# Sliding-window attention and channel mix on one core: another order of the three compute engines' lists

## The chip, the cores and the metric

The kernel runs on one core of one Trainium2 chip. The core has a matrix engine (PE), a vector engine (DVE), a scalar engine (ACT), a general engine (POOL) and a sync engine (SP). Each takes its own list of instructions in order and waits at the head of it. Here POOL and SP mostly issue DMA transfers. The metric is the time of one execution on the device in microseconds (us).

## What is computed

Attention over 8 batches, 8 heads, 576 positions and 64 values per head, with a linear bias by distance and a window of 128 positions; its output, with the heads side by side, goes through a channel mix with a hidden width of 1024.

```python
scores = scale * np.matmul(q, k.transpose(0, 1, 3, 2))
rel = pos[:, None] - pos[None, :]
bias = slopes[:, None, None] * (-np.abs(rel).astype(np.float32))[None, :, :]
mask = (rel >= 0) & (rel < window)
scores = np.where(mask, scores + bias[None], -1000000000.0)
attn = np.exp(scores - np.max(scores, axis=-1, keepdims=True))
attn = attn / (np.sum(attn, axis=-1, keepdims=True) + 1e-09)
x = np.matmul(attn, v)                    # then (B, S, H * D)
x_prev = np.concatenate([np.zeros((B, 1, D)), x[:, :-1, :]], axis=1)
xk = mu_k * x + (1.0 - mu_k) * x_prev
xr = mu_r * x + (1.0 - mu_r) * x_prev
k = np.maximum(xk @ w_k, 0.0)
v = k * k @ w_v
return 1.0 / (1.0 + np.exp(-(xr @ w_r))) * v
```

The multiplications take bf16 and sum in f32.

## The kernel before

**Attention.** A batch is worked in head pairs, numbered 0 to 3 in the text (g in the code). For each pair q and k are transposed, on PE (L398, out of qx or cb, with the identity ident or its f32 form id) or by DMA (L554, qx out of cb), and where PE does it a copy (L715) on ACT or DVE brings the result from PSUM to a buffer qk. PE computes scores for two heads (L742). In batch 0 the bias is added on PE by multiplying dist, the table of distances, with sid, a scaled identity per head (L748; DVE makes the eight sids at L687); from batch 1 on DVE multiplies with a mask instead (L779; the mask is made by ACT at L1198). ACT takes the exponential (L766, into at). PE multiplies with v and a column of ones (L395, vs or tv with at: the "attend"), and DVE divides (L813, L819, into xu). That result is transposed, on PE with a copy (L398, L715 into xt) or by DMA on SP (L928, xt out of xu), and DVE forms the shifted mixes (L906 into dl, L913 into xk and xr). Batch 0 is worked in two halves, so that PE has its first work early: four pairs of 768-wide exponentials for the first half, then the second half, whose scores have a 768-wide and a 512-wide part.

**Channel mix.** Two batches are 1152 rows, and they are worked in chunks of 512, 384 and 256 columns, the first of all in two chunks of 256. For each of eight groups of the hidden width PE multiplies xk with wk_sb (L395), ACT takes the relu (L1022, into rl), and DVE, or ACT in the early chunks, squares it (L996 and L994, into kk). For each 128 rows PE multiplies xr with wr_sb, ACT takes a tanh (L1040, into rs), PE multiplies kk with wv_sb, and DVE joins both (L1054, into one of five buffers ot), from where SP sends 256 KB out (L1079).

**Loads.** POOL issues nearly all loads in one fixed list: v, q, k, then wk_sb in two halves, further batches, wr_sb and wv_sb in two halves (L560). Only the first q and k of pairs 0 and 1 come through SP and ACT (L569, into qx), and DVE casts them (L715 CAST qx).

**PSUM.** There are eight banks, in four pairs (duo0 to duo3). One of them first holds the output of 82 small multiplications of a cleared buffer (L395, duo out of warm), which have no use but to keep PE at work; they are steps in PE's list like the others.

**What sets the order.** The program describes every piece of work as a step with its engine or engines, the steps it depends on, the buffers it takes and those it gives back. Each step for PE, ACT or DVE gets the next number when it is added, and a table ORDER holds for each of these engines the numbers in the order in which they are to run. Where a step may run on ACT or on DVE (many copies L715, the early squares), the list in which its number stands decides.

```python
        self.places = {n: (e, i) for e, ns in ORDER.items() for i, n in enumerate(ns)}
```

A run through all steps then takes for such an engine only the step that is next in its list (`n.place == turn[e]`) and gives it free buffers. POOL and SP take, of the steps that are ready in that run, the first by a written priority, so their lists follow from the others. The program is emitted in that order, and the chip's engines wait for each other by semaphores.

Of the kernel before, what the change touches and what calls it, by code (L numbers as in the profile page):

```python
# [20 lines left out]

ORDER = {
    "PE": [int(x) for x in """
# [17 lines left out]
""".split()],  # L41
    "ACT": [int(x) for x in """
# [11 lines left out]
""".split()],  # L54
    "DVE": [int(x) for x in """
# [16 lines left out]
""".split()],  # L72
}

# [1249 lines left out]
```

## Time and profile before

| What | Value |
|---|---|
| runs | median 227.4 us of 3 (226.96 to 227.56) |
| the profiled execution | 226.97 us |
| its span | 225.1 us; 1.87 us lie around it |
| busy | PE 217.7, DVE 186.8, ACT 153.0, POOL 91.9 us |
| last work of PE | ends 3.3 us ahead of the span's end |
| granted clock of PE | full in all 40 slices |

The span is the time that the trace covers. A row of a timeline gives the start in us from the span's start, how long the group took from first start to last end, engine, line, operation, what it writes and reads, the shape and the count; at its end, in brackets, how long the engine stood idle before and for what. Neighbouring groups of PE overlap in the rows, since its multiplications are pipelined: a start that follows soon after the last start is no loss.

### The profile page before, as it was taken

How to read it: one execution, taken by the hardware profiler on the slowest of the kernel's cores; microseconds unless marked ns; L12 is line 12 of the kernel's file. 1: busy time of each engine (PE TensorE's matmuls, PEld its weight loads, DVE VectorE, ACT ScalarE, POOL GpSimd, SP SyncE). 2: the span in 40 equal slices, each digit the busy share in tenths (PEclk: the TensorE clock that was granted, in tenths of full speed). 3: DMA queues.
4: the chain of work that ended last, by engine and by line, in shares of the span. 5: the costliest groups of instructions: out<-in, count | busy, mean ns of one | idle time of the engine just before them, and what ended most of it. 6: DMA issues, size and time to landing. Idle time of an engine off the chain costs nothing.

```text
span 225.1 us, 6344 instructions
## 1 busy us (share of the span) xinstructions
PE 217.7 (97%) x2525; PEld 131.5 (58%) x2555; DVE 186.8 (83%) x422; ACT 153.0 (68%) x276; POOL 91.9 (41%) x118
## 2 busy tenths in 40 slices
PE   8999999999999999999999999999999999999994
PEld 8666756756765555555665565446664655456542
DVE  5779898899768998999789996599969989957433
ACT  2488999898999886980899665843469654135801
POOL 8865726589980983374428663400000000000000
PEclk9999999999999999999999999999999999999999
DMA  7999999999999999999999999999952121243015
GB/s 169 177 186 200 195 197 175 227 146 178 185 154 148 161 149 156 150 182 133 207 207 142 152 181 155 148 180 191 206 167 76 51 57 30 79 155 126 3 41 192
DMA packets 132093, 33.85 MB, mean 150 GB/s; under 512 B 119256, under 2 KB 127712, under 8 KB 132064
## 3 DMA queue, kind: packets, MB, share of 16 engines
q0 software_dynamic: 95728, 16.26, 96.5%
q1 hardware_dynamic: 34592, 16.59, 36.6%
q10 hardware_dynamic: 1744, 0.59, 1.1%
q8 instruction: 20, 0.33, 0.6%
q14 instruction: 9, 0.07, 0.1%
HBM read 33.56 MB, written 9.44 MB: 191 GB/s over the span
## 4 chain that ended last, share of the span: by engine, by line
PE 91%; ACT 4%; DVE 2%; issue 1%; DVEq 0%
PE duo L395 77%; PE duo L742 7%; PE duo L398 4%; PE duo L748 2%; ACT at L766 1%; ACT xt L715 1%; ACT rl L1022 1%; ACT qk L715 1%; DVE ot L1054 1%; DVE qk L715 1%; ACT kk L994 0%; DVE at L779 0%; ACT rs L1040 0%; DVE tv L499 0%; DVE tt L715 0%
## 5 line engine op out<-in xcount | busy, mean ns | idle before, releaser
L1022 ACT ACTIVATE rl<-duo 128x256 bf16<-128x256 f32 (+2 forms) x104 | 47.3, 485 | 34.8 <-PE duo L395 25.1
L395 PE MATMUL duo<-xk,wk_sb 128*128 128x256 bf16 (+2 forms) x410 | 70.2, 312 | 0.3
L766 ACT ACTIVATE at<-duo 128x1024 bf16<-128x1024 f32 (+2 forms) x68 | 63.8, 987 | 8.9 <-PE duo L742 8.5
L395 PE MATMUL duo<-wv_sb,kk 128*128 128x512 bf16 (+2 forms) x281 | 66.1, 373 | 1.1 <-issue 0.5
L395 PEld LDWEIGHTS <-wk_sb 128*128 128x128 bf16 x416 | 38.9, 98 | 22.9 <-issue 0.8
L395 PEld LDWEIGHTS <-kk 128*128 128x128 bf16 x296 | 27.1, 98 | 29.8 <-issue 1.3
L779 DVE TENSOR_TENSOR at<-at,mask 128x1024 bf16<-128x1024 bf16 x56 | 37.2, 680 | 5.8 <-ACT at L766 5.7
L519 POOL DMA_DIRECT2D vs<-in_v_dram x32 | 28.4, 901 | 22.7 <-PE duo L395 16.8
L996 DVE TENSOR_TENSOR kk<-rl 128x256 bf16<-128x256 bf16 (+2 forms) x95 | 29.9, 336 | 8.4 <-ACT rl L1022 8.3
L395 PE MATMUL duo<-wr_sb,xr 128*128 128x512 bf16 x135 | 35.5, 379 | 0.5
L1040 ACT ACTIVATE rs<-duo 128x512 bf16<-128x512 f32 x36 | 21.6, 612 | 19.8 <-PE duo L395 17.1
L1054 DVE SCALAR_TENSOR_TENSOR ot<-rs,duo 128x512 f32<-128x512 bf16 (+2 forms) x37 | 24.3, 665 | 9.1 <-PE duo L395 8.9
L819 DVE TENSOR_TENSOR xu<-duo,rc 128x640 bf16<-128x640 f32 (+2 forms) x36 | 26.2, 738 | 0.4
L913 DVE SCALAR_TENSOR_TENSOR xk<-dl,mu_sb,xt 128x576 bf16<-128x576 bf16 (+1 forms) x32 | 24.6, 779 | 0.2
L913 DVE SCALAR_TENSOR_TENSOR xr<-dl,mu_sb,xt 128x576 bf16<-128x576 bf16 (+1 forms) x32 | 24.6, 778 | 0.0
L395 PEld LDWEIGHTS <-at 128*128 128x128 bf16 x576 | 21.5, 97 | 4.8 <-issue 0.3
L395 PE MATMUL duo<-vs,at 128*128 128x65 bf16 x512 | 21.7, 193 | 0.0
L395 PEld LDWEIGHTS <-xr 128*128 128x128 bf16 x144 | 13.3, 98 | 12.9 <-issue 0.4
L550 POOL DMA_DIRECT2D cb<-in_k_dram x20 | 17.8, 926 | 7.3 <-DMA vs<-in_v_dram 7.2
L550 POOL DMA_DIRECT2D cb<-in_q_dram x20 | 17.7, 931 | 5.6 <-DMA vs<-in_v_dram 2.5
L715 ACT COPY qk<-duo 128x512 bf16<-128x512 bf16 (+1 forms) x25 | 14.5, 593 | 0.4 <-PE duo L398 0.4
L906 DVE TENSOR_TENSOR dl<-xt 128x576 bf16<-128x576 bf16 (+1 forms) x32 | 13.4, 438 | 1.1 <-ACT xt L715 0.6
(73 smaller groups left out, 189.4 us busy)
## 6 DMA issues: line engine op xcount, KB each, us to landing
out_dram<-ot SPq DMA_DIRECT2D x34, 256.0 KB, 4.7
vs<-in_v_dram POOLq DMA_DIRECT2D x32, 128.0 KB, 8.5
cb<-in_q_dram POOLq DMA_DIRECT2D x20, 128.0 KB, 9.8
cb<-in_k_dram POOLq DMA_DIRECT2D x20, 128.0 KB, 11.2
wk_sb<-in_moe_w_k_dram POOLq DMA_DIRECT2D x2, 512.0 KB, 8.7
cb<-in_q_dram POOLq DMA_DIRECT2D x4, 256.0 KB, 9.7
cb<-in_k_dram POOLq DMA_DIRECT2D x4, 256.0 KB, 9.7
wv_sb<-in_moe_w_v_dram POOLq DMA_DIRECT2D x2, 512.0 KB, 12.2
```

What stands on the lines that cost most here:

```text
L395: return use(h, nc.tensor.matmul(*a, **k))
L519: return dma(POOL, 256, issue_t(1024), lambda e: nc.gpsimd.dma_start(out=vs_buf[h.idx][:, j, :, 0:D], in_=v[b, :, 128 * j:128 * j + 128].r ...
L550: return [dma(POOL, 256, issue_t(1024), lambda e, r=r: nc.gpsimd.dma_start(out=cb_buf[h.idx][:, i, r], in_=src[:, :, r]), [g], kind="q") f ...
L715: return (nc.scalar.copy if e == ACT else nc.vector.tensor_copy)(out=out, in_=in_)
L766: lambda e, ah=ah, w=w, hp=hp: nc.scalar.activation(out=ah(), in_=two(hp)[:, :, 0:w], func=AF.Exp, scale=float(scale)), (), [hp])
L779: nc.vector.tensor_tensor(out=a, in0=a, in1=m, op=ALU.mult)
L819: use(hp, nc.vector.tensor_tensor(out=out_, in0=a5()[:, :, :, 0:D], in1=rc[:, :, 0:nt, None].to_broadcast([128, 2, nt, D]), op=ALU.mult), hx)
L913: lambda e: nc.vector.scalar_tensor_tensor(out=buf[hk.idx][:, g, e0 + c0:e0 + c1], in0=dls(), scalar=mu[:, g:g + 1], in1=xc(1), op0=ALU.mu ...
L996: nc.vector.tensor_tensor(out=out, in0=in_, in1=in_, op=ALU.mult)
L1022: a = op(ACT, act_t(n), [s], pr, lambda e, hp=hp, hr=hr: use(hp, nc.scalar.activation(out=rl_buf[hr.idx][:, 0:n], in_=one(hp)[:, 0:n], fun ...
L1040: lambda e, hp=hp, hs=hs: use(hp, nc.scalar.activation(out=rs_buf[hs.idx], in_=one(hp), func=AF.Tanh, scale=0.5), hs), [hs], [hp])
L1054: use(hv, nc.vector.scalar_tensor_tensor(out=ot_buf[ho.idx][:, a:b], in0=rs_buf[hs.idx][:, a:b], scalar=1.0, in1=one(hv)[:, a:b], op0=ALU. ...
```

## The change

Only the table ORDER is another. It has the same 451 numbers for PE in another order, and for ACT and DVE the same 703 between them in another order; 15 steps have changed engine: seven from DVE to ACT (five copies of q and k, among them those of pair 1 and pair 3 in the first half of batch 0, and two squares) and eight from ACT to DVE (six copies of q and k, among them that of pair 2 there and one of batch 1, and two squares). The rest of the program is line for line the same. POOL's list of loads is the same; in SP's list some output transfers and DMA transposes have changed places. The number of fillers ahead of PE's first transposes is 47, where it was 46.

The start of PE's list in the table (one line of thirteen of it):

```diff
 ORDER = {
     "PE": [int(x) for x in """
-84 109 92 74 83 70 64 40 43 115 97 106 59 80 62 102 110 47 81 100 50 65 105 91 117 103 60 77 93 49 79 112 72 63
+95 88 43 115 65 56 54 84 53 104 96 119 110 68 62 118 82 44 90 52 105 116 87 74 41 81 107 77 86 72 71 112 111 55
```

What this does is seen in the engines' instructions (output, inputs and shape; buffers carry their number and the allocator's).

DVE, first half of batch 0, before: one sid among clearings (L499) and the copies of q and k of pair 3 (into qk1) and pair 1 (into qk3).

```order
L715 CAST qk1_72<-duo3_126 128x2x256
L499 MEMSET tv1_66 64x8x65
L687 TENSOR_SCALAR sid_115<-ident_112 128x128
L499 MEMSET at3_80 128x64
L715 COPY qk3_74<-duo3_126 128x2x256
```

DVE, after: the beginning of the list, up to the first cast of q and k.

```order
L483 MEMSET vs0_63 128x32
L462 TENSOR_SCALAR ident_112<-dist_114 128x128
L687 TENSOR_SCALAR sid_115<-ident_112 128x128 x3
L685 COPY dist_114<-dist_114 128x256
L698 CAST id32_121<-ident_112 128x128
L687 TENSOR_SCALAR sid_115<-ident_112 128x128 x2
L483 MEMSET vs1_64 128x32
L687 TENSOR_SCALAR sid_115<-ident_112 128x128
L715 CAST qx0_75<-qx1_76 128x2x2x64
```

All sids but one, the first copy of dist and the cast of the identity stand ahead of the first cast of q and k; before, one sid stood ahead of it and the last one behind a clearing of tv.

ACT, the first exponentials of batch 0 (at0, at1, at2 for pairs 0, 3 and 2, then at0 for pair 1), before:

```order
L766 ACTIVATE at0_77<-duo1_124 128x2x384
L715 CAST qk2_73<-duo1_124 128x2x256
L766 ACTIVATE at1_78<-duo0_123 128x2x384
L766 ACTIVATE at2_79<-duo1_124 128x2x384
L766 ACTIVATE at0_77<-duo2_125 128x2x384
L715 COPY qk1_72<-duo1_124 128x2x128
```

ACT, after:

```order
L766 ACTIVATE at0_77<-duo0_123 128x2x384
L715 CAST qk1_72<-duo3_126 128x2x256
L766 ACTIVATE at1_78<-duo1_124 128x2x384
L766 ACTIVATE at2_79<-duo0_123 128x2x384
L715 COPY qk3_74<-duo3_126 128x2x256
L766 ACTIVATE at0_77<-duo2_125 128x2x384
L715 COPY xt0_89<-duo3_126 128x256
```

The cast between the first two exponentials is that of pair 3 (into qk1) instead of pair 2 (into qk2), and the copy of pair 1 (qk3) stands on ACT behind pair 2's exponential; DVE has pair 2's cast in exchange.

ACT, the second half of batch 0 (the first row is pair 0's 768-wide part; at0 then holds pair 3's 512-wide one, at1 pair 0's, at2 pair 1's two parts and at3 pair 2's), before:

```order
L766 ACTIVATE at1_78<-duo1_124 128x2x384
L766 ACTIVATE at0_77<-duo3_126 128x2x256
L766 ACTIVATE at1_78<-duo2_125 128x2x256
L766 ACTIVATE at2_79<-duo1_124 128x2x384
L766 ACTIVATE at2_79<-duo0_123 128x2x256
L766 ACTIVATE at3_80<-duo3_126 128x2x384
L1198 ACTIVATE mask_113<-dist_114 128x256
L766 ACTIVATE at3_80<-duo0_123 128x2x256
```

ACT, after:

```order
L766 ACTIVATE at1_78<-duo1_124 128x2x384
L766 ACTIVATE at0_77<-duo2_125 128x2x256
L1198 ACTIVATE mask_113<-dist_114 128x256
L766 ACTIVATE at1_78<-duo3_126 128x2x256
L766 ACTIVATE at2_79<-duo1_124 128x2x384
L766 ACTIVATE at2_79<-duo2_125 128x2x256
L1198 ACTIVATE mask_113<-dist_114 128x256
L766 ACTIVATE at3_80<-duo0_123 128x2x384
L766 ACTIVATE at3_80<-duo1_124 128x2x256
```

Table steps (L1198) now stand ahead of pair 0's 512-wide part and ahead of pair 2's two parts, where one stood between those two; on PE the second scores of pair 0 stand directly behind their bias, and the last scores of pair 2 ahead of the attend of pair 1, where they stood behind it.

SP, the transposes of batch 7 (L928 into xt1) and the output transfers around them, before:

```order
L1079 DMA out_0_dram<-ot0_107 128x512
L1079 DMA out_0_dram<-ot1_108 128x512
L928 DMA_TRANSPOSE xt1_90<-xu0_85 128x5x128
L928 DMA_TRANSPOSE xt1_90<-xu1_86 128x5x128
L928 DMA_TRANSPOSE xt1_90<-xu0_85 128x5x128 x2
L1079 DMA out_0_dram<-ot0_107 128x512
L1079 DMA out_0_dram<-ot1_108 128x512
```

SP, after:

```order
L1079 DMA out_0_dram<-ot0_107 128x512 x2
L928 DMA_TRANSPOSE xt1_90<-xu0_85 128x5x128
L1079 DMA out_0_dram<-ot0_107 128x512
L928 DMA_TRANSPOSE xt1_90<-xu1_86 128x5x128
L928 DMA_TRANSPOSE xt1_90<-xu0_85 128x5x128
L928 DMA_TRANSPOSE xt1_90<-xu1_86 128x5x128
L1079 DMA out_0_dram<-ot0_107 128x512
```

One output transfer now stands between the first and the second transpose; the other three follow it.

84 rows, old and new, of the table ORDER are left out of this document.

## The prediction

> **What bounds the kernel now.** I read the busy shares first, then the busy time by stretch, then the timelines of PE, ACT and DVE where PE is not full. The first row is the page's busy share of PE; the others are the busy times in stretches of the span (start:end, length, busy us and instructions of each engine, granted clock, DMA share, GB/s).
>
> ```profile
> PE 217.7 (97%) x2525; PEld 131.5 (58%) x2555; DVE 186.8 (83%) x422; ACT 153.0 (68%) x276; POOL 91.9 (41%) x118
> ...
> 5.36:12.00 6.64, 6.37 (x86) 4.53 (x84) 5.08 (x21) 2.99 (x5) 5.42 (x8) 1.00 1.81 180
> 12.00:20.00 8.00, 7.68 (x177) 4.88 (x175) 6.71 (x26) 6.88 (x17) 5.10 (x7) 1.00 1.59 191
> 20.00:30.00 10.00, 9.52 (x244) 7.97 (x243) 9.31 (x28) 9.89 (x26) 6.44 (x8) 1.00 1.43 198
> 40.00:100.00 60.00, 59.14 (x869) 35.72 (x877) 53.80 (x108) 53.67 (x97) 41.25 (x50) 1.00 1.93 167
> 100.00:160.00 60.00, 59.48 (x573) 34.09 (x582) 53.05 (x107) 38.02 (x63) 24.27 (x30) 1.00 1.78 170
> 160.00:221.80 61.80, 61.33 (x457) 34.36 (x462) 46.47 (x100) 30.38 (x57) 0.00 (x0) 1.00 0.32 94
> 221.80:225.10 3.30, 0.02 (x1) 0.00 (x0) 0.43 (x2) 0.00 (x0) 0.00 (x0) 1.00 0.35 120
> ```
>
> PE is the bound: 97% busy, at granted clock 1.00 in every stretch. From 40 us to its last matmul it stands idle 0.86 + 0.52 + 0.47 = 1.85 us, and that is all another order could save there. Late in the kernel its matmuls start at one interval:
>
> ```profile
> 100.55 3.62 PE L395 MATMUL duo<-wv_sb,kk 128*128 128x512 bf16 x16
> ```
>
> Sixteen in 3.62 us, the last of which lasts about 0.38, are one per (3.62 - 0.38)/15 = 0.216 us, with no hole. The same multiplications stand in both lists, so this body cannot shrink; only the holes can. They lie ahead of 30 us, where three engines hand work back and forth and the fillers (L395 out of warm) take up what is left. PE's timeline there (start, length, work, idle before and what ended it):
>
> ```profile
> 8.10 0.33 PE L395 MATMUL duo<-warm 128*128 128x128 bf16 x3
> 8.30 0.65 PE L398 MATMUL duo<-id,qx 128*128 128x128 f32 x4
> ...
> 9.61 0.22 PE L395 MATMUL duo<-warm 128*128 128x128 bf16 x1
> 10.10 0.50 PE L748 MATMUL duo<-dist,sid 128*128 128x384 bf16 x2 [0.27 <-DVE at L499]
> 10.53 0.34 PE L742 MATMUL duo<-qk 64*128 64x256 bf16 x4
> ...
> 11.50 0.34 PE L742 MATMUL duo<-qk 64*128 64x256 bf16 x4
> ...
> 11.89 0.34 PE L395 MATMUL duo<-vs,at 128*128 128x65 bf16 x6
> ```
>
> At 10.10 the bias of head pair 2 (L748) waits. DVE's timeline says for what: its sid (L687) stands behind a clearing of 0.49 us.
>
> ```profile
> 8.30 0.69 DVE L715 CAST qk<-duo 128x512 bf16<-128x512 f32 x1 [0.30 <-PE duo L398]
> 9.16 0.49 DVE L499 MEMSET tv<- 64x520 bf16 x1 [0.17 <-issue]
> 9.66 0.38 DVE L687 TENSOR_SCALAR sid<-ident 128x128 bf16<-128x128 bf16 x1
> ```
>
> ACT is idle between its first exponentials and again later in batch 0; it waits for PE's scores:
>
> ```profile
> 7.43 0.81 ACT L766 ACTIVATE at<-duo 128x768 bf16<-128x768 f32 x1 [3.19 <-PE duo L742]
> 8.99 0.58 ACT L715 CAST qk<-duo 128x512 bf16<-128x512 f32 x1 [0.75 <-PE duo L398]
> 9.49 0.81 ACT L766 ACTIVATE at<-duo 128x768 bf16<-128x768 f32 x1
> 10.91 0.81 ACT L766 ACTIVATE at<-duo 128x768 bf16<-128x768 f32 x1 [0.61 <-PE duo L742]
> ...
> 14.68 0.81 ACT L766 ACTIVATE at<-duo 128x768 bf16<-128x768 f32 x1 [0.20 <-PE duo L742]
> ...
> 19.24 2.49 ACT L766 ACTIVATE at<-duo 128x512 bf16<-128x512 f32 x4 [0.48 <-PE duo L742]
> ```
>
> After that ACT is full (9.89 of 10 us from 20 to 30), and PE waits for its copies (the first row is the last attend of batch 0):
>
> ```profile
> 22.64 0.44 PE L395 MATMUL duo<-vs,at 128*128 128x65 bf16 x9
> ...
> 26.83 0.79 PE L398 MATMUL duo<-ident,cb 64*64 64x64 bf16 x47
> 27.82 0.32 PE L398 MATMUL duo<-ident,cb 64*64 64x64 bf16 x17 [0.20 <-issue]
> 28.39 0.39 PE L742 MATMUL duo<-qk 64*128 64x256 bf16 x4 [0.25 <-ACT qk L715]
> 28.72 0.44 PE L398 MATMUL duo<-ident,cb 64*64 64x64 bf16 x32
> ```
>
> **The change, term by term.** Nothing is added or removed: the same steps run, 15 of them on the other of ACT and DVE. So each term is a wait that goes or comes, worked out by laying the rows' durations along the new lists.
>
> *To 12 us: -0.3.* All multiplies for sid but one now stand ahead of DVE's first cast, so the wait at 10.10 goes: from 9.61 to 10.10 PE did one filler, which is 0.4 us lost. Of the four copies of q and k, that of head pair 3 goes from DVE to ACT, directly behind the first exponential, whose end is 7.43 + 0.81 = 8.24; with its 0.58 us it is done by 8.9, which the idle 0.75 us at 8.99 covers. That of head pair 2 goes from ACT to DVE: the three fillers at 8.10 no longer stand between the two groups of f32 transposes, so the second runs at about 8.10 + 0.65 = 8.75, and the copy at 8.75 + 0.69 = 9.45. So its scores start at 9.5 instead of 10.53 and its exponential follows at 9.49 + 0.69 = 10.2 instead of 10.91, with its attend at 11.0 instead of 11.89. Against this, head pair 1's copy now stands on ACT behind that exponential (10.85 to 11.4), so its scores stay at 11.5. A wait of about 0.1 us of the attend for that exponential is new; queued behind it on PE are fillers and pair 1's scores, which wait for their copy until 11.5 anyway. 0.4 less 0.1 is 0.3; the ends are 0 (the fillers only move) and 0.5.
>
> *12 to 24 us: -0.5.* PE now does head pair 0's second scores directly behind their bias, and the last scores of pair 2 before, not behind, the attend of pair 1. ACT's wait of 0.48 at 19.24 goes; the one at 14.68 grows from 0.20 to about 0.5, since those scores come at the same time but ACT arrives earlier. That is 0.48 - 0.3, about 0.2, on ACT. PE itself is idle for 8.00 - 7.68 = 0.32 us in this stretch, and since its list no longer puts a step that must wait ahead of one that is ready at these two places, I count that as gone: 0.2 + 0.3 = 0.5. Ends: 0 and 0.8 (0.48 + 0.32). The last attend of batch 0 should then start 0.8 earlier than 22.64.
>
> *26 to 29 us: -0.3.* From 26.83 to 28.72 PE does 64 transposes and 4 scores. At the rate of the row behind, 32 in 0.44 us, the transposes take 0.88 us, and the scores 0.33 (28.39 to 28.72): 0.7 us of the 1.89 are lost to ACT's copies. One copy and one square leave ACT's list near here for DVE, and PE puts the scores ahead of the last two groups of transposes; I let 0.3 of the 0.7 go, less than half, for DVE is 9.31 of 10 us full and can take little. Ends: 0 and 0.6.
>
> *The gate at 35 us: +0.3.* The first matmuls on the second half of wv cannot come before its load. POOL's list is row for row the same, so this load is issued when it was.
>
> ```profile
> L560 POOL DMA_DIRECT2D wv_sb<-in_moe_w_v_dram x2: 740/742/745, 20.1 to 21.7; - x2
> ...
> DMA to landing us min/median/max: 11.2/12.2/13.1
> 35.64 1.03 PE L395 MATMUL duo<-wv_sb,kk 128*128 128x512 bf16 x4
> ```
>
> Issued at 21.7, after 13.1 us, it is there at 34.8; its consumer starts at 35.64. So no more than 0.8 us of lead passes this place, and 0.3 + 0.5 + 0.3 = 1.1 is cut to 0.8. Ends: 0 (PE fills in with other work in the new order) and +0.3.
>
> *Behind 36 us: -0.3.* Of the 1.85 us idle the new lists remove, by the durations, some waits of scores for a free PSUM bank. I take 0.3; the ends are -0.9 (half of all that is there) and +0.6 (new waits of the same kind; nothing in the profile excludes them).
>
> *The end: 0.* Behind the last matmul stand 3.30 us of multiply and output transfer, the same in both. One more filler ahead of the first transposes is (0.33 - 0.22)/2 = 0.06 us, by the three in the row at 8.10, which the terms' rounding holds.
>
> The sum is -0.3 - 0.5 - 0.3 + 0.3 - 0.3 = -1.1 us. The profiled execution took 226.97 us (span 225.1 and 1.87 around it), so about 225.9. The median of the runs, 227.4, lies 0.43 above that execution, so the forecast for the median is 226.3 us.
>
> **Rivals.**
>
> *The lead is given back (227.2).* Term three rests on ACT, and term four shows one load that clips. If ACT takes as long as before from 20 to 30 us (it holds the same exponentials, and its list is one step shorter in 281), the first two terms are lead that ACT's full stretch eats, and of the rest I leave -0.2: 227.4 - 0.2 = 227.2. For it speaks 9.89 of 10; against it that ACT starts this stretch earlier, since waits ahead of it shrink.
>
> *The port (226.9).* The sids now run while POOL issues its first loads, and some multiplies are slow there:
>
> ```profile
> L687 DVE TENSOR_SCALAR sid<-ident x8: 174/298/556, 1.6 to 9.7; 128x128 bf16<-128x128 bf16 x8
> ...
> 3.43 0.68 DVE L715 CAST qx<-qx 128x256 bf16<-128x256 f32 x1 [1.61 <-DMA qx<-in_q_dram]
> ...
> 2.09 1.91 POOL L519 DMA_DIRECT2D vs<-in_v_dram  x2
> ...
> 5.36 0.39 PE L398 MATMUL duo<-ident,qx 128*128 128x128 bf16 x4
> ```
>
> A slow one costs 556 - 174 = 0.38 us more. DVE's idle 1.61 us covers four of them, and PE needs the casts only at 5.36, which is 1.25 behind the first one's end (3.43 + 0.68), less some 0.3 for the second: 0.9. If all seven were slow, and the copy of dist and the cast of the identity that are moved ahead with them, 9 x 0.38 = 3.4 us stand against 2.5, and 0.9 is lost. The middle one of the eight takes 298 ns, so not all are slow: I price it at 0.6, and 226.3 + 0.6 = 226.9. The Trainium skill, "SBUF — State Buffer", section "Who interferes with whom", speaks for this case: a copy, cast or tensor_scalar of DVE in a two-port mode and GpSimd exclude each other, and the one that issues second "fully blocks". This trace agrees as far as multiplies of 174 and of 556 ns stand side by side in it; by the rule taken alone all seven would be slow, and the time would be the 227.2 of 0.9 us lost.
>
> *Slower: batch 7's transposes on SP (228.7).* SP's list follows, and one output transfer now stands between the first and the second of batch 7's four transposes (L928). What they bring is used soon:
>
> ```profile
> 181.37 7.76 SPq L928 DMA_TRANSPOSE xt<-xu  x3
> ...
> 186.03 0.45 DVE L906 TENSOR_TENSOR dl<-xt 128x576 bf16<-128x576 bf16 x1
> ...
> xt<-xu SPq DMA_TRANSPOSE x12, 3.8
> ```
>
> By the median of 3.8 us to landing there is 186.03 - 181.37 - 3.8 = 0.9 us to spare at present, and by the new lists about 0.7. If the transfer ahead, or a late output buffer that it waits for, holds the second transpose for over 0.7 us, DVE stops at L906, with the squares for the next matmuls behind it. A transpose that takes as long to land as the issue of those three (7.76) comes 4.0 us late, 3.3 of it beyond the spare; four ready matmuls on PE (4 x 0.216) cover 0.9, and 2.4 are lost: 226.3 + 2.4 = 228.7. It decides from 1.8 lost on. Against it: the last of the four is now issued earlier, for its attend is.
>
> *More than forecast (225.3).* If the gate does not clip (+0.3 falls away) and the idle time behind 36 us halves (0.9 instead of 0.3): 226.3 - 0.9 = 225.4, and with term two at its end 225.1; 225.3 between them.
>
> **Chances.** About 0.3% (0.7 us) is what a measurement of this kernel can tell from no change: below 226.7 is faster, above 228.1 is slower. Forecast 0.58 (its own range 225.8 to 226.9, so 0.54 of it faster, 0.04 the same); lead given back 0.17; port 0.04; SP 0.13; more 0.08. Faster 0.54 + 0.08 = 0.62, the same 0.04 + 0.17 + 0.04 = 0.25, slower 0.13. The range from 225.4 to 227.6 takes in the first three cases and part of the last, and leaves out SP's and some of the rest.
>
> **What the profile of the changed kernel would show.** Right: no wait of L748 for L499 near 10 us; the third 768-wide exponential at about 10.2; no idle time of ACT near 19; the last 65-wide group of batch 0 at about 21.8; the second half of wv used at about 34.9; PE's last matmul about 1.1 us ahead of 221.8. Wrong: sids of over 500 ns in a row and first transposes later than 5.5; PE waits for ACT's copies near 27 us that sum to 0.7 again; wv's load landing later than 34.8, since it is paced by what the queue holds; DVE waiting at L906 behind 186 us. The forecast fails above all if loads or transposes take other times than before, for these I carried over unchanged.

## The result

| | Before | After |
|---|---|---|
| runs | 227.42 us median of 15 (226.95 to 227.82) | 226.27 us median of 15 (225.46 to 226.76) |
| ratio | | 0.995, 95% interval 0.9941 to 0.9959 |
| profiled execution | 226.97 us, span 225.1 | 226.72 us, span 224.9 |

The changed kernel is 1.15 us faster in the median; the forecast was 1.1, and 226.3 for the median. The two profiled executions alone show only 0.25, and that is the first thing to explain: the one of before lies near the lowest of its runs, the one of after near the highest of its own. Later runs of the same kernel give other profiles, which are used below.

The page of after, and its busy times in the stretches read before (columns as there):

```profile
PE 217.6 (97%) x2524; PEld 133.1 (59%) x2555; DVE 187.4 (83%) x423; ACT 151.3 (67%) x275; POOL 92.0 (41%) x118
```

```profile
5.36:12.00 6.64, 6.60 (x80) 5.24 (x79) 2.72 (x12) 3.40 (x6) 5.42 (x8) 1.00 1.81 179
12.00:20.00 8.00, 7.90 (x177) 5.40 (x179) 7.18 (x28) 6.88 (x17) 5.11 (x7) 1.00 1.58 192
20.00:30.00 10.00, 9.41 (x249) 7.80 (x244) 9.61 (x30) 9.85 (x26) 6.27 (x8) 1.00 1.44 198
```

PE is fuller from 5.36 to 20 us and ACT as full as before from 20 to 30. PE's timeline in the head, of after:

```profile
5.98 0.63 PE L398 MATMUL duo<-ident,qx 128*128 128x128 bf16 x4
...
8.01 0.34 PE L742 MATMUL duo<-qk 64*128 64x256 bf16 x4
8.28 0.50 PE L748 MATMUL duo<-dist,sid 128*128 128x384 bf16 x2
8.62 1.04 PE L398 MATMUL duo<-id,qx 128*128 128x128 f32 x8
9.49 0.49 PE L748 MATMUL duo<-dist,sid 128*128 128x384 bf16 x2
9.81 0.28 PE L395 MATMUL duo<-warm 128*128 128x128 bf16 x2
10.02 0.34 PE L742 MATMUL duo<-qk 64*128 64x256 bf16 x4
10.29 0.23 PE L395 MATMUL duo<-warm 128*128 128x128 bf16 x1
10.46 0.34 PE L742 MATMUL duo<-qk 64*128 64x256 bf16 x4
```

The last bias (9.49) follows at once: the wait for a sid is gone. The two groups of f32 transposes are one row of eight. But the first transposes start at 5.98 instead of 5.36, though only one filler more stands ahead of them: in this execution the fillers ran at half rate, one per 0.107 us, until about 6.7 us, where in that of before one per 0.056 began at 4.75. ACT's timeline of after:

```profile
8.39 0.81 ACT L766 ACTIVATE at<-duo 128x768 bf16<-128x768 f32 x1 [2.62 <-PE duo L742]
9.25 0.58 ACT L715 CAST qk<-duo 128x512 bf16<-128x512 f32 x1
10.40 1.51 ACT L766 ACTIVATE at<-duo 128x768 bf16<-128x768 f32 x2 [0.56 <-PE duo L742]
11.80 0.59 ACT L715 COPY qk<-duo 128x512 bf16<-128x512 bf16 x1
13.06 0.81 ACT L766 ACTIVATE at<-duo 128x768 bf16<-128x768 f32 x1 [0.67 <-ACT qk L715]
...
15.97 0.81 ACT L766 ACTIVATE at<-duo 128x768 bf16<-128x768 f32 x1 [0.45 <-PE duo L742]
...
17.99 1.30 ACT L766 ACTIVATE at<-duo 128x768 bf16<-128x768 f32 x2
...
19.48 1.85 ACT L766 ACTIVATE at<-duo 128x512 bf16<-128x512 f32 x3
```

Pairs 3 and 2 are one row now (10.40), the wait of 0.48 near 19 us is gone, and the one ahead of the second half's first exponential has grown from 0.20 to 0.45. New is 0.67 at 13.06: pair 1's scores wait for the copy that ACT itself made at 11.80. Between 24 and 36 us, PE of after:

```profile
25.58 1.92 PE L395 MATMUL duo<-xk,wk_sb 128*128 128x256 bf16 x16
27.88 0.39 PE L742 MATMUL duo<-qk 64*128 64x256 bf16 x4 [0.38 <-ACT rl L1022]
28.36 1.01 PE L398 MATMUL duo<-ident,cb 64*64 64x64 bf16 x64
```

The waits for ACT have not gone; they have changed place, from the transposes to the scores ahead of them, and from ACT's copies to its relus.

**Where the time went, by PE's list.** For each profile I added up the time that PE's matmuls take at full rate along its list and took it from the time at which each starts. The full rate is 0.216 us per 512 columns, and 0.095 us for a change between matmuls that use 128 rows and 64 rows of PE: in the second profile of after, 64-row scores behind a matmul of 512 columns start 0.311 us after it, not 0.216. What grows between two moments is time that PE lost. Against the profile of before, in us (negative is less lost):

| Profile | 12 to 24 us | 24 to 36 | 36 to 80 | 80 to the end |
|---|---|---|---|---|
| after, first profile | -0.61 | +0.06 | -0.01 | -0.33 |
| after, second profile | -0.71 | +0.07 | -0.02 | -0.33 |
| three other profiles with the old head and old middle | -0.15, -0.15, 0 | +0.01 each | 0 (two of them) | 0 (one) |

So about 0.6 come from 12 to 24 us, 0.3 behind 80 us, and nothing from between. The repeats of the old lists say that 0.15 is scatter.

A second reading needs no such sum. At some places both lists have done the same steps of PE: at its 122nd, 158th and 236th (about 20, 36.6 and 79 us), and at its 449th, close to the end. The time between two such places, from the start of the step behind the one to the start of the step behind the other, can be compared as it stands, in us:

| Profile | 122nd to 158th step | 158th to 236th | 236th to 449th |
|---|---|---|---|
| before | 16.65 | 42.64 | 141.97 |
| after, first and second profile | 16.77, 16.78 | 42.47, 42.47 | 141.64, 141.64 |

The new list makes one change of rows more ahead of the 158th step and one fewer behind it, 0.095 us each, which is most of the 0.12 and half of the 0.17. The 0.33 at the end stand as in the sum. How early PE is at its 122nd step depends on when the first loads land, and comes up with the fillers below.

### The profile page after: what moved, and what is told of

It is laid out like the page before. It is cut to its first block, busy times and chain, and to the rows that moved or that the text cites. A ratio compares the mean times of both kernels' runs of the same rounds, so it can differ in the third digit from the quotient of the medians.

```text
span 224.9 us, 6343 instructions
## 1 busy us (share of the span) xinstructions
PE 217.6 (97%) x2524; PEld 133.1 (59%) x2555; DVE 187.4 (83%) x423; ACT 151.3 (67%) x275; POOL 92.0 (41%) x118
## 4 chain that ended last, share of the span: by engine, by line
PE 90%; ACT 6%; issue 2%; DVE 0%; DVEq 0%; ACTq 0%
PE duo L395 77%; PE duo L742 7%; PE duo L398 3%; PE duo L748 2%; ACT at L766 2%; ACT rl L1022 1%; ACT qk L715 1%; ACT xt L715 1%; ACT rs L1040 1%; ACT mask L1198 0%; ACT kk L994 0%; DVE ot L1054 0%; DVE rc L813 0%; DVEq L1319 0%; DVE warm L488 0%
## 5 line engine op out<-in xcount | busy, mean ns | idle before, releaser
L1022 ACT ACTIVATE rl<-duo 128x256 bf16<-128x256 f32 (+2 forms) x104 | 46.8, 483 | 32.0 <-PE duo L395 23.8
L996 DVE TENSOR_TENSOR kk<-rl 128x256 bf16<-128x256 bf16 (+2 forms) x95 | 30.5, 335 | 8.2 <-ACT rl L1022 7.9
L715 ACT COPY xt<-duo 128x640 bf16<-128x640 bf16 (+3 forms) x24 | 13.4, 578 | 2.5 <-PE duo L398 2.4
L906 DVE TENSOR_TENSOR dl<-xt 128x576 bf16<-128x576 bf16 (+1 forms) x32 | 13.6, 437 | 0.7 <-ACT xt L715 0.3
```

The costliest lines, as they stand in the source:

```text
L715: return (nc.scalar.copy if e == ACT else nc.vector.tensor_copy)(out=out, in_=in_)
L996: nc.vector.tensor_tensor(out=out, in0=in_, in1=in_, op=ALU.mult)
L1022: a = op(ACT, act_t(n), [s], pr, lambda e, hp=hp, hr=hr: use(hp, nc.scalar.activation(out=rl_buf[hr.idx][:, 0:n], in_=one(hp)[:, 0:n], fun ...
```

## The experiments

Each kernel was timed beside the kernel before on the same chip; median, range and ratio (with its 95% interval) stand below each.

### New lists to 20 us, to 36 us, and old lists to 36 us

At PE's 122nd, 158th and 236th step (20, 36.6 and 79 us) both lists have done the same steps but for one or two of ACT and DVE, so one can go on with the other. The first kernel, h20, has the table of the changed kernel up to the first of these and the old one behind:

```diff
 ORDER = {
     "PE": [int(x) for x in """
-84 109 92 74 83 70 64 40 43 115 97 106 59 80 62 102 110 47 81 100 50 65 105 91 117 103 60 77 93 49 79 112 72 63
+95 88 43 115 65 56 54 84 53 104 96 119 110 68 62 118 82 44 90 52 105 116 87 74 41 81 107 77 86 72 71 112 111 55
...
+108 214 109 234 97 91 235 177 197 157 237 145 183 184 238 217 186 187 200 203 201 218 204 240 189 267 206 220
 221 243 279 223 192 273 264 276 209 340 226 261 258 270 328 361 343 373 295 326 313 287 331 282 376 334 364 284
```

> The lists of the changed kernel up to its 122nd step of PE (about 20 us: batch 0's scores and their fillers), the old lists behind it. My theory: the first two terms (-0.3 and -0.5) are made here and pass the load of wv, since 0.8 is what it lets through: 0.7 to 0.8 us under the kernel before, about 226.7, with the last attend of batch 0 some 0.8 us earlier where the clock rises at the same moment. Rival, the lead is given back to ACT's full stretch and the load: within 0.2 of before, 227.2 to 227.4. Rival, all gain stands behind 36 us: 227.4.

227.68 us (227.36 to 227.99), ratio 1.0009 (0.9999 to 1.002): not faster, if anything slower, and above the times of both rivals. PE's timeline of this kernel shows where the gain goes:

```profile
21.22 0.32 PE L395 MATMUL duo<-vs,at 128*128 128x65 bf16 x5
21.84 0.29 PE L395 MATMUL duo<-vs,at 128*128 128x65 bf16 x4 [0.30 <-ACT at L766]
```

In the midst of pair 1's attend PE waits for its exponential, 0.46 us by the sum above, and from 24 to 36 us another 0.2 is lost. From its 122nd to its 158th step PE takes 17.33 us, more than with either full list. The old list behind 20 us asks for things in an order for which this ACT list has not made them.

h36 goes on with the new table to 36.6 us:

```diff
+279 243 273 223 192 258 209 267 340 226 328 264 261 276 270 343 373 361 313 295 326 331 282 287 364 334 376 284
 289 301 290 346 367 379 285 298 292 304 349 337 382 310 321 370 352 316 307 481 318 385 502 484 467 323 319 487
```

> The lists of the changed kernel up to PE's 158th step (about 36.6 us), the old lists behind it. My theory: all terms but the one behind 36 us, -0.3 - 0.5 - 0.3 + 0.3 = -0.8: about 226.6; if the load of wv does not clip, -1.1: 226.3. Rival, the stretch from 26 to 29 us gives nothing: the same as the kernel with the first 20 us changed. Rival, the gain stands behind 36 us: 227.2 to 227.4.

227.30 us (226.76 to 227.70), ratio 0.999 (0.9979 to 1.0). By PE's list the 0.7 from 12 to 24 us is there, but behind the seam stands a wait that neither parent has:

```profile
38.29 1.47 PE L395 MATMUL duo<-xk,wk_sb 128*128 128x256 bf16 x12
39.98 0.62 PE L395 MATMUL duo<-vs,at 128*128 128x65 bf16 x15 [0.22 <-ACT at L766]
```

Twelve matmuls of 256 columns at 0.108 are 1.30 us, so 0.38 of the 1.69 to the attend are lost. From the 158th to the 236th step this kernel takes 43.05 us, 0.4 more than before. The 0.15 measured is 0.6 less the seam's 0.4; the time is that of the rival that sees the gain behind 36 us, but not for its reason.

t36 has the old table to 36.6 us and the new one behind:

```diff
-289 301 290 346 367 379 285 298 292 304 349 337 382 310 321 370 352 316 307 481 318 385 502 484 467 323 319 487
+289 301 290 346 367 379 285 292 298 304 310 349 337 370 321 382 352 316 481 318 307 385 484 502 323 467 319 487
```

> The old lists up to PE's 158th step, those of the changed kernel behind it. My theory: the term behind 36 us alone, -0.3: about 227.1. Rival, the gain stands there: 226.3 to 226.6. Rival, the late part gives nothing or has new waits: 227.4 or more.

227.17 us (226.63 to 227.36), ratio 0.9983 (0.9973 to 0.9993): -0.28, as the last term said. From the 236th to the 449th step it takes 141.57 us, as the new lists do; from the 158th to the 236th it takes 42.67, so it has lost 0.2 against them at its seam.

### One sid earlier

```diff
-... 26 22 18 162 17 32 24 138 129 167
+... 26 22 18 32 162 17 24 138 129 167
```

(DVE's list; 32 is the last sid, 162 pair 3's cast, 17 the clearing of tv.)

> The kernel before with one number moved in DVE's list: the last sid, on which the bias of pair 2 waited at 10.10 us, stands ahead of pair 3's cast and of the clearing of tv. My theory: PE's wait of 0.27 at that bias goes, pair 2's scores start by 0.3 to 0.4 earlier, and the time falls by 0.2 to 0.3: about 227.2. Rival, PE only does its fillers sooner and pair 2's scores then wait for ACT's copy: the bias is early, the time within 0.1 of before, 227.4.

227.29 us (226.50 to 227.76), ratio 0.9992 (0.998 to 1.0004): -0.16, not to be told from nothing. PE's timeline of this kernel:

```profile
9.24 0.40 PE L398 MATMUL duo<-ident,qx 128*128 128x128 bf16 x4
9.47 0.22 PE L395 MATMUL duo<-warm 128*128 128x128 bf16 x1
9.53 0.49 PE L748 MATMUL duo<-dist,sid 128*128 128x384 bf16 x2
9.95 0.34 PE L742 MATMUL duo<-qk 64*128 64x256 bf16 x4
```

The wait is gone and nothing takes its place; what it is worth lies between 0 and 0.45 us.

### The changed kernel again, seams at 79 us, and fewer fillers

> The changed kernel once more, beside the others. In its first profile the fillers ran at half rate until 6.65 us, where the four profiles of the first runs switch between 4.04 and 4.49 and that of the kernel before at 4.75, and pair 2 and 3's transposes started at 8.62. My theory: that was chance, and in another execution the rate rises ahead of 5 us; the f32 transposes then start when the last of the eight first loads lands (7.5 to 8.6 us in the six profiles). Median 226.0 to 226.5, PE's lost time by 12 us at 0.1 to 0.4 under that of the kernel before for the same landing. Rival, the changed head makes the rate rise late each time: a switch behind 6 us again.

The same kernel again: 226.35 us (225.99 to 226.77), ratio 0.9956 (0.9944 to 0.9969). The fillers ran at half rate until 6.19 us, but so did they in the three other profiles taken on that chip, until 5.87 (which has the old head), 5.98 and 6.40: the order does not set the moment. The page's wait rows of this second profile:

```profile
PE duo L395 <- DVE warm L488: 1.0, 1, 1.0
PE duo L742 <- ACT rl L1022: 0.4, 1, 0.4
```

Only the wait at 27.6 us is left besides the start.

h79 changes over at 79 us, from the new table to the old; t79 from the old to the new:

```diff
+430 526 595 472 431 423 475 586 613 420 436 425 478 426 454 457 618 493 589 421 462 459 627 630 621 460 464 592
 538 553 544 624 633 541 550 547 598 636 465 564 569 745 754 574 601 535 727 748 556 559 757 730 604 576 561 571
```

```diff
-538 553 544 624 633 541 550 547 598 636 465 564 569 745 754 574 601 535 727 748 556 559 757 730 604 576 561 571
+550 544 553 633 624 541 547 538 598 636 465 564 569 601 754 745 574 535 727 748 757 556 559 730 604 561 576 562
```

> The lists of the changed kernel up to PE's 236th step (about 79 us), the old ones behind it. My theory now: in the kernels with a seam at 20 and at 36 us the gain from 12 to 24 us (0.5 to 0.6 in the profiles) was made, and some 0.4 given back at the seam, where engines stand at other points than the list behind it was made for; at 79 us the two orders agree but for one step, so it is kept: 0.8 to 0.9 under before, 226.6. Rival, the first 36 us are worth 0.15 as measured, and only the late part brings gain: 227.2.

> The old lists up to PE's 236th step, those of the changed kernel behind it. My theory: the late gain, which the profiles place between 160 and 180 us, -0.3 to -0.4: 227.1. Rival, the two parts gain only together, and each alone 0.1 to 0.2: 227.3.

h79: 226.71 us (226.51 to 226.89), ratio 0.9971 (0.9961 to 0.9982). Without a wait at the seam the first part is worth 0.7 of the 1.1. t79: 227.48 us (227.30 to 227.81), ratio 1.0004 (0.9995 to 1.0013): the late part, which brought 0.28 in t36, brings nothing here, and again there is a wait at the seam, 0.41 us by the sum:

```profile
79.78 1.67 PE L395 MATMUL duo<-wv_sb,kk 128*128 128x512 bf16 x7
81.70 0.62 PE L395 MATMUL duo<-vs,at 128*128 128x65 bf16 x15 [0.24 <-ACT at L766]
```

The three kernels that fell short of their parts have such a wait of 0.4 to 0.5 us; of the two that did not, t36 loses 0.2 at its seam and h79 nothing.

nf12 leaves out 12 of the 47 fillers ahead of the first transposes:

```diff
-        plan.add(PE, 0.118 if i < 40 else 0.056, 0.0, [n_warm, g_wm], (1e12, i), emit_warm, (), [h_wm])
+        skip = plan.placed in (39, 50, 51, 57, 60, 76, 93, 100, 106, 114, 117, 120)
+        plan.add(PE, 0.001 if skip else 0.118 if i < 40 else 0.056, 0.0, [n_warm, g_wm], (1e12, i),
+                 None if skip else emit_warm, (), [h_wm])
```

> The changed kernel without 12 of the 47 fillers ahead of the first transposes (they have no use for the result). The first casts end at 4.3 us, the transposes start behind the fillers at 5.0 to 6.0. Theory, the first loads set the head: the transposes start at 4.75, the f32 ones when their load lands, and the time falls by 0.2 at most: 226.0 to 226.3. Rival, the fillers hold the head: 0.5 to 0.8 less, 225.6. Third, with fewer fillers the rate rises later and the time is 0.3 or more above the changed kernel.

226.47 us (225.99 to 226.50), ratio 0.9959 (0.9945 to 0.9972): no other than the changed kernel, and a little above the first theory. The number of fillers does not hold the head: the profile of nf12 is 0.42 us ahead of the second one of after at PE's 122nd step (19.50 against 19.92), but its first loads had also landed 0.45 earlier. What holds it where the load is late is seen in an execution of the old head (t36), where PE stands in the f32 transposes:

```profile
7.47 0.27 PE L398 MATMUL duo<-id,qx 128*128 128x128 f32 x1
8.35 0.55 PE L398 MATMUL duo<-id,qx 128*128 128x128 f32 x3 [0.60 <-DMA qx<-in_q_dram]
```

The last of the eight first loads landed between 7.49 and 8.62 us in the profiles of all these kernels, early and late with either head. By the sum, with the load late, the old head has lost 3.92 us by 12 us where it landed at 8.47 (t36); the new one 3.78 at the same 8.47, and 3.74 at 8.52. That is some 0.15 us better up to 12 us, no more than the scatter. Up to PE's 122nd step, with the stretch from 12 to 20 us in it, the new lists are 0.4 to 0.65 us better: after's second profile, h36, h79 and h20, with the load at 8.47 to 8.62, are there at 19.88 to 20.05, t36 at 20.53 and m8b (8.51, described below) at 20.46. With the load early there is one pair, before (7.86, 122nd step at 19.95) and the first profile of after (7.88, at 20.20), and it does not show the order's share: in after the fillers' rate rose 2 us later, and PE came to the f32 transposes only at 8.62, without a wait.

### The table steps early, and one piece of PE's order

m8 puts ACT's eight table steps ahead of its first exponential, in the changed kernel; m8b does the same in the kernel before.

```diff
-10 11 12 13 14 127 162 165 153 138 141 170 182 181 232 132 215 236 199 158 146 253 185 239 252 188 202 205 250
+10 11 12 13 14 248 249 250 251 252 253 254 255 127 162 165 153 138 141 170 182 181 232 132 215 236 199 158 146
...
-    ms = [op(ACT, act_t(256, True), [n_dist] + gate, (2, h), lambda e, h=h: make_mask(h))
+    ms = [op(ACT, act_t(256, True), [n_dist], (2, h), lambda e, h=h: make_mask(h))
```

> The changed kernel with ACT's eight table steps (L1198) ahead of its first exponential, where it stands idle for 2.3 us, instead of among the work of 17 to 31 us (they need only dist; the dependency that holds them back is taken out). From 24 to 36 us PE waits 1.1 to 1.3 us in every profile, in both orders, mostly for ACT's copies and relus. My theory: ACT is what holds that stretch, so 8 x 0.3 = 2.4 us less on ACT there takes away most of these waits: 0.6 to 1.0 under the changed kernel, about 225.5, unless the load of wv then clips (34.0 landed, used at 35.7: 1.7 us to spare). Rival, the stretch is held by DVE or by the order of the lists: no more than 0.2 gained.

> The same move of the eight table steps in the kernel before. My theory: the same 0.6 to 1.0 under the kernel before, 226.4 to 226.8, clipped where wv lands at 34.8 with 0.8 us to spare: the two orders then still lie about 0.5 to 1.0 apart. Rival: 227.3 and more.

m8: 226.02 us (225.64 to 226.39), ratio 0.9938 (0.9925 to 0.9952). m8b: 226.98 us (226.35 to 227.69), ratio 0.9984 (0.9972 to 0.9996). That is 0.25 to 0.45 us less in the median by either order, half of what was expected; for m8 the interval still meets that of the changed kernel. From its 122nd to its 158th step PE takes 16.45 us in m8, 0.32 less than in after; in m8b it takes 16.66, no less than before, and where the gain of m8b lies its profile does not show. ACT and PE of m8:

```profile
4.19 2.56 ACT L1198 ACTIVATE mask<-dist 128x256 bf16<-128x256 bf16 x8
8.47 0.81 ACT L766 ACTIVATE at<-duo 128x768 bf16<-128x768 f32 x1 [1.72 <-PE duo L742]
...
24.86 0.38 ACT L1022 ACTIVATE rl<-duo 128x256 bf16<-128x256 f32 x1 [0.61 <-PE duo L395]
```

```profile
28.50 0.39 PE L742 MATMUL duo<-qk 64*128 64x256 bf16 x4 [0.80 <-ACT rl L1022]
```

The table steps cost nothing where they stand now, but the time they free on ACT turns into ACT's wait for PE at 24.86, and PE still waits for ACT at 28.50. So the amount of work on ACT is not the whole limit there; that the rest is the order in which the two engines ask is what the last kernel below tests.

g0s2 has the old table with the one piece of PE's list that the forecast named for 12 to 24 us:

```diff
-... 186 237 238 203 200 201 187 217 204 218 240 189 267 206 220 221 243
+... 186 237 238 187 203 200 201 217 204 218 240 189 220 221 267 206 243
```

> The kernel before with one piece of PE's list in the changed order: pair 0's second scores directly behind their bias, and pair 2's last scores ahead of the attend of pair 1. My theory, as in the second term: ACT's wait of 0.48 at 19.24 us goes, the last attend of batch 0 comes 0.3 earlier: 227.1. Rival: what gains from 12 to 24 us is the order of the transposes and biases ahead of that (waits at 13.51, 15.54 and 17.25 us, 0.6 together), and this piece is worth nothing: 227.4.

227.40 us (226.62 to 227.98), ratio 1.0 (0.9989 to 1.0011): the rival's time. In its profile ACT has no wait near 19 us any more, but PE gains only 0.1: from its 80th to its 122nd step it takes 8.80 us, against 8.89 to 8.90 in the four profiles whose lists are the old ones there (before, t36, t79, sid32). At 29.18 us PE then waits 1.0 (row of its page's waits):

```profile
PE duo L398 <- issue: 1.0, 1, 1.0
```

m8b has the same wait (1.01 us at 28.91). It looks like the place where a gain is given back, but it is not: from the 122nd to the 158th step PE takes 16.67 us here, and 16.65 to 16.66 in those four, where the waits are spread. This profile loses another 0.25 us between 180 and 182 us, which the others do not, and no run tells why.

### One step more

m8p is m8 with batch 1's first scores ahead of the last group of xk multiplications:

```diff
-279 243 273 223 192 258 209 267 340 226 328 264 261 276 270 343 373 361 313 295 326 331 282 287 364 334 376 284
+279 243 273 223 192 258 209 267 340 226 328 264 261 276 343 270 373 361 313 295 326 331 282 287 364 334 376 284
```

> The changed kernel with the table steps early and one step of PE moved: batch 1's first scores (L742, which waited 0.8 us at 28.5 for a PSUM bank that ACT's relus free) stand ahead of the last group of xk multiplications instead of behind it, so that one bank fewer is taken when they start. My theory: what is left of the wait from 24 to 30 us is the order of these lists, and about 0.3 of the 0.8 go: 225.7. Rival, the second half of wv (landed 34.2, used at 35.8 with the table steps early) or another wait behind takes it back: 226.0, as without the move.

225.58 us (225.39 to 226.18), ratio 0.9922 (0.9907 to 0.9938), the fastest of all, 0.7 us under the changed kernel, and its interval lies below that kernel's. It is 0.4 under m8 in the median, but on another chip, and their intervals still meet. PE's timeline:

```profile
24.98 1.48 PE L395 MATMUL duo<-xk,wk_sb 128*128 128x256 bf16 x12
26.39 0.40 PE L742 MATMUL duo<-qk 64*128 64x256 bf16 x4
26.73 0.61 PE L395 MATMUL duo<-xk,wk_sb 128*128 128x256 bf16 x4
27.27 1.15 PE L398 MATMUL duo<-ident,cb 64*64 64x64 bf16 x64
```

The scores start without a wait, and from its 122nd to its 158th step PE takes 16.27 us, against 16.45 in m8 and 16.65 in before. This was one step in one list, and no engine has less to do than in m8.

## Why the prediction came out, point by point

**The sum, -1.1, was right; two of its five steps were not, and they cancelled.** That the median came within 0.05 us of the forecast is in part luck.

*To 12 us, -0.3: the mechanism was right, the size at most half.* The wait for the sid is gone in every profile of the new head, and pairs 3 and 2 run on without a gap. But the rows of one profile had been taken for the rule. With the old head too the wait is missing in two profiles (t79 and g0s2), where the first transposes came at 5.87 and 5.88 us instead of 5.36. And where the first loads land late, f32 transposes and all behind them wait in both orders, and the new one is 0.15 ahead. Pair 1's scores were said to come when they did; in the new head ACT waits 0.67 for them.

*12 to 24 us, -0.5: the size was about right (0.6 to 0.7 by the sum; 0.4 to 0.65 up to PE's 122nd step, the head included), the reason half.* The wait near 19 us went, and the one at 14.68 grew to 0.45 where about 0.5 was said. But the piece of PE's list that the step named brought PE 0.1 in g0s2 and nothing in the time. The rest may be the order of transposes and biases ahead of it, that the step didn't speak of; that is argued from the table, since no kernel had that part alone. Nor does any kernel keep the 15 steps on their old engines and change only the order, so what these 15 are worth is open.

*26 to 29 us, -0.3: wrong.* PE lost 0.06 more by the sum, not 0.3 less, from 24 to 36 us. The step let a copy and a square that leave ACT shorten PE's wait; the wait went to another place. That the amount of work on ACT was not the whole limit is what m8 and m8p show: 2.4 us less on ACT gave 0.25 to 0.45 in the median, and one step moved on PE 0.4.

*The gate at 35 us, +0.3: wrong as well.* The load was said to be issued when it was. POOL's list is the same, but POOL waits too, for earlier loads to land (1.5 us for one of wk_sb and 0.6 for one of cb), and in the first profile of after it issued the two loads later:

```profile
L560 POOL DMA_DIRECT2D wv_sb<-in_moe_w_v_dram x2: 740/742/745, 20.7 to 22.0; - x2
...
DMA to landing us min/median/max: 11.0/11.6/12.2
```

By 22.0 + 12.2 it was there at 34.2, and PE came for it at 35.95. In the second profile of after it was issued at 23.0 and there at 35.2, and PE came at 35.69. So the load landed up to 0.6 us earlier and 0.4 later than was said, and PE did not wait for it; m8p, which is further ahead, uses it at 34.78 without a wait. The two terms together say 0, and +0.06 was measured.

*Behind 36 us, -0.3: right,* 0.33 behind 80 us in both profiles of after, and 0.28 in the time of t36. The rows of the scores of batch 7 say how, before and in the second profile of after:

```profile
171.63 0.38 PE L395 MATMUL duo<-wv_sb,kk 128*128 128x512 bf16 x1
171.94 0.71 PE L742 MATMUL duo<-qx 64*128 64x256 bf16 x8
...
173.10 0.59 PE L395 MATMUL duo<-wv_sb,kk 128*128 128x512 bf16 x2 [0.16 <-issue]
```

```profile
171.76 0.34 PE L742 MATMUL duo<-qx 64*128 64x256 bf16 x4
...
172.53 1.04 PE L395 MATMUL duo<-wv_sb,kk 128*128 128x512 bf16 x4
```

The scores there took from 171.94 to 173.10, 1.16 us, part of which is a hole of 0.22 that a missing record leaves, and take 0.77. That is 0.17 less; the scores at 142 us bring another 0.14 (0.92 and 0.78 us to the multiplications behind them). The bound for this term was read too freely. Most of the 1.85 us idle from 40 us on were such holes, not waits: the second profile of after, whose 2555 records are whole, shows 0.12 in the first of the three stretches and none in the others. m8b, whose records are whole too and whose lists are the old ones there, shows 0.17 there and none in the others. So the 0.33 were gained where the rows show PE busy throughout: its records overlap, and a multiplication that starts late does not show as idle time.

```profile
40.00:100.00 60.00, 59.88 (x883) 35.99 (x881) 54.97 (x109) 52.61 (x95) 41.89 (x51) 1.00 2.04 168
100.00:160.00 60.00, 60.00 (x585) 34.26 (x583) 52.48 (x106) 37.56 (x61) 24.15 (x29) 1.00 1.79 171
```

*The end, 0: right.*

**The rivals.** "The lead is given back" is what h20, h36 and t79 did, where new and old lists meet; in the changed kernel itself, whose lists fit each other, it did not happen. The port did not decide: the sids took as the row says

```profile
L687 DVE TENSOR_SCALAR sid<-ident x8: 180/279/606, 1.4 to 4.6; 128x128 bf16<-128x128 bf16 x8
```

Three of the eight took 431 to 606 ns, and all three end within 0.1 us of the end of POOL's first issue of vs (2.10 to 3.12 us); one inside that issue, at 2.27, took 186. The Trainium skill, "SBUF — State Buffer", section "Who interferes with whom", says that a tensor_scalar of DVE in a two-port mode and GpSimd exclude each other and that the second to issue "fully blocks"; this trace agrees for the three and not for the fourth. The casts still begin at 3.46, for DVE's idle time ahead of them (1.61 us in before) covered it. Three signs that were to show the forecast wrong came all the same: sids of over 500 ns in a row, first transposes later than 5.5 (from the fillers' rate), and, in the second profile, wv's load later than 34.8. None of them cost what it was to stand for. On SP, batch 7's second transpose was issued at 186.04 instead of 183.73, by more than the 0.7 us that the rival allowed, and the first step behind them came later:

```profile
xt<-xu SPq DMA_TRANSPOSE x12, 5.4
```

```profile
190.40 0.82 DVE L906 TENSOR_TENSOR dl<-xt 128x576 bf16<-128x576 bf16 x2
```

The median landing, 5.4 us where the forecast had read 3.8, is over twelve transposes of three batches; batch 7's own, where the trace has them, took 2.57 us twice before, and 2.55 and 4.07 after. L906 came at 190.40 instead of 186.03, but DVE had other work ahead of it and no idle time at that row, and PE lost nothing there.

## What to carry over

Orders of several engines are worth more together than by parts: a piece that removes a wait brought nothing that the time shows, and a seam between two good orders cost 0.2 to 0.5 us in four of five kernels. So a forecast for a moved step should follow the gain to the next place where two engines wait for each other in turn, and ask there in which order they ask, not only how much work each has. To compare two orders, take the time between places where both have done the same steps. And the load queue is no fixed clock: its issues wait for earlier loads to land, and one profile shows one landing of it.

## What was not expected of the hardware

The moment at which the fillers change from one per 0.107 to one per 0.056 us lay between 4.04 and 7.03 us in the profiles, with PE busy from 0.99 us on, and the rows of the two profiles read here give a granted clock of 1.00 in that stretch too. The Trainium skill, "TensorE: Matmul & The Clock Gate", section "Part 1: The HAM clock gate", says that PE starts at half rate and that the window which decides is free-running, so the moment varies from run to run; these profiles agree, but where the section gives that variation as ±500 ns, they spread over 3 us. The landing of the first loads, 7.49 to 8.62 us, varied by as much, and no run here tells why.
